# Forgetting attention with a channel mix on one core: norms of the first pairs spread by a selection matmul, a new layout for the later norms' trip, first mix from slot 5

## The chip, the cores and the metric

One core of one Trainium2 chip runs the whole program. The metric is the device time of one execution in microseconds. Runs are marked fast or slow by their time and clock. A ratio is the mean time of one kernel's fast runs over the mean time of the other's fast runs of the same rounds, so it is not quite the ratio of the medians that I quote: those are over all runs of a kernel, slow ones too. In the traces PE is TensorE's matmuls (PEld its weight loads), DVE is VectorE, ACT ScalarE, POOL GpSimd, and SPq the queue that issues the transfers.

## The reference, cut to what matters

```python
# q, k, v: (8 batches, 8 heads, 576, 64); f: (8, 8, 576)
scores = q @ k.T / 8 + cum[:, None] - cum[None, :]     # cum = cumsum(log(clip(f, 1e-4, 1)))
scores = where(causal, -1e9, scores)
x = softmax(scores) @ v                                # -> (8, 576, 512)
xk, xr = mixes of x and x shifted by one row (mu_k, mu_r)
out = sigmoid(xr @ w_r) * (relu(xk @ w_k) ** 2 @ w_v)  # (8, 576, 512), float32
```

The kernel folds the decay into v and into the softmax sums. What is left of the softmax is a division by a sum for each query, which is done on the way from PSUM to x.

## The kernel before

Heads are taken in 32 pairs. The main loop has 35 slots. Slot s computes the scores of pair s, the sums of pair s-1 and the values of pair s-3, with pieces of the channel mix in between. The sums of two pairs gather in one PSUM tile `den`. A "norm" turns the sums of such a group of two pairs into reciprocals R: 128 partitions of 288 values, of which two rows in every 32 are used. To scale x, each row must be spread over 64 partitions. This is done by a trip through DRAM:

```python
def norm(g):                       # after the sums of pairs 2g and 2g+1
    dT = dT_ring()
    nc.vector.transpose(dT..., den[:, 0:HQ])
    nc.vector.reciprocal(rt[:, :, 0:2], dT[:, :, 0:2])
    nc.vector.transpose(R..., rt...)

def spread_norm(g):                # scr: DRAM [4, 32, HQ]; HQ = 288
    scr = scr_ring()
    nc.sync.dma_start(out=scr.rearrange("g r c -> (g r) c"), in_=R.rearrange("p a b -> p (a b)"))
    rb = rb_ring()
    for half in range(2):
        for hh in range(2):
            nc.sync.dma_start(
                out=rb[hh * D:(hh + 1) * D, :, half * HQ:(half + 1) * HQ],
                in_=scr[2 * half + hh, 0:2, :].unsqueeze(0).to_broadcast([D, 2, HQ]))
    for i in range(2):
        rbs[2 * g + i] = rb[:, i, :]

def values(Pi, half):
    nm = mm_ring()                 # three PSUM buffers, shared with the mix
    ...                            # matmuls a x vw into nm
    nc.vector.tensor_tensor(out=xs[...], in0=nm[:, 0:HQ], in1=rbs[Pi][:, o:o + HQ], op=ALU.mult)
```

The channel mix comes in key units (x times w_k, `run_keys`, which take a buffer of the same `mm_ring`) and in gate and value blocks (w_r and w_v, `run_gv`). The order within a slot, cut:

```python
for s in range(NP + LAG):
    ...                            # loads
    scores(s, 0); mask(s, 0); scores(s, 1); mask(s, 1); mask(s, 4)
    run_gv(value_unit)
    transposes(s + 1)
    run_keys(2 * more)
    scores(s, 2); scores(s, 3); ...
    denominators(s - 1)
    values(Pi, 0); values(Pi, 1)   # Pi = s - 3
    ...
    if s % 2 == 0: norm(s // 2 - 1)
    run_keys(2 * more)
    if s % 2 == 0: spread_norm(s // 2 - 1)
    shift(Pi); run_gv(); ...
```

The softmax here doesn't subtract the row's maximum and nothing guards it: scores larger than these inputs give would overflow.

Of the kernel before, what the change touches and what calls it, by code (L numbers as in the profile page):

```python
# [9 lines left out]
F32 = mybir.dt.float32  # L10
# [18 lines left out]
HQ = 288  # L29
# [3 lines left out]
def kernel(  # L33
# [49 lines left out]
    scr_ring = Ring(2, [4, 32, HQ], F32, "scr", drp)  # L83
# [14 lines left out]

    NQ, NV = 3, 3
    qf = [cp.tile([P, 4, 2, D], F32, name=f"qf{i}") for i in range(NQ)]  # L100
    kf = [cp.tile([P, 4, 2, D], F32, name=f"kf{i}") for i in range(NQ)]
# [5 lines left out]
    def load(src, t, Pi, eng=None):  # L107
        b, h0 = divmod(2 * Pi, H)
        for hh in range(2):
            (eng or nc.sync).dma_start(  # L110
                out=t[:, :, hh, :],
                in_=src[b, h0 + hh, :4 * P, :].rearrange("(c p) d -> p c d", p=P))

    def load_qk(Pi):
        load(q, qf[Pi % NQ], Pi)
        load(k, kf[Pi % NQ], Pi)

    def load_v(Pi):
        load(v, vf[Pi % NV], Pi)

    def load_tail(i, b, eng=None):
        (eng or nc.sync).dma_start(out=tail_f[i],
                                   in_=(q, k, v)[i][b, :, 4 * P:, :].rearrange("h p d -> p h d"))

    for tt in tail[0] + tail[1]:
        nc.vector.memset(tt[64:, :, :], 0.0)
    for tt in tail[2]:
        nc.gpsimd.memset(tt[64:, :, :], 0.0)
# [4 lines left out]
    load_tail(0, 0)  # L133
    load_tail(1, 0, nc.scalar)
    nc.scalar.dma_start(out=lf, in_=f_bh[:, :])
    load_qk(1)
    mu_k_sb = cp.tile([P, n_db], F32)
# [3 lines left out]
    load_qk(2)  # L141
# [5 lines left out]
    make_identity(nc, ident32)  # L147
    NQK = 2
# [7 lines left out]
    nc.vector.memset(rt, 0.0)  # L156
    nc.gpsimd.memset(R, 0.0)
    den = dnp.tile([P, 512], F32)
# [10 lines left out]
    def cast_pair(Pi):  # L169
        res = []  # L170
        for ring, src in ((qb_ring, qf[Pi % NQ]), (kb_ring, kf[Pi % NQ])):
            t = ring()
            eng = nc.vector if Pi < 2 else nc.gpsimd
            eng.tensor_copy(t, src.rearrange("p c h d -> p c (h d)"))  # L174
            res.append(t)
        casts[Pi] = res

    def cast_tails(b):
        for i in range(2):
            eng = nc.vector if b == 0 else nc.gpsimd  # L180
            eng.tensor_copy(tail[i][b % 2][:64], tail_f[i])
# [13 lines left out]
    def transposes(Pi):  # L195
        b, p = divmod(Pi, PRW)
        tp = sc_ring().bitcast(BF16)
        for i, src in enumerate(casts.pop(Pi)):
            for c in range(NC):
                in_ = src[:, c, :] if c < 4 else \  # L200
                    tail[i][b % 2][:, 2 * p:2 * p + 2, :].rearrange("p h d -> p (h d)")
                nc.tensor.transpose(tp[:, i, c * P:(c + 1) * P], in_, ident)  # L202
        nc.vector.tensor_copy(qkT[Pi % NQK], tp[:, :, 0:640])  # L203

    cast_pair(0)
    cast_tails(0)
    transposes(0)



    ref = cp.tile([BH, 1], F32)
    nc.vector.memset(zrow, 0.0)
    nc.vector.tensor_scalar(lf, lf, scalar1=1e-4, scalar2=1.0, op0=ALU.max, op1=ALU.min)
    nc.scalar.activation(out=lf, in_=lf, func=AF.Ln)
    nc.vector.tensor_tensor_scan(out=cum, data0=lf, data1=zrow, initial=0.0,
                                 op0=ALU.add, op1=ALU.add)
    nc.vector.tensor_scalar(ref, cum[:, S - 1:S], scalar1=0.5, scalar2=None, op0=ALU.mult)
    nc.scalar.activation(out=wrow, in_=cum, func=AF.Exp, bias=ref, scale=-1.0)
    wtp = sc_ring()[:, 0, 0:NC * BH].rearrange("p (c h) -> p c h", c=NC)
    for c in range(NC):  # L220
        sz = P if c < 4 else 64
        nc.tensor.transpose(wtp[:sz, c, :], wrow[:, c * P:c * P + sz], ident32)
    nc.vector.tensor_copy(wbf[:, :4, :], wtp[:, :4, :])
    nc.vector.tensor_copy(wbf[:64, 4, :], wtp[:64, 4, :])


    for hh in range(2):
        for c in range(NC):
            nc.vector.tensor_copy(
                E[:, c, :].rearrange("p (g x) -> p g x", x=8)[:, :, hh * 2:hh * 2 + 6:5],  # L230
                wbf[:, c, :].rearrange("p (g h) -> p g h", h=4)[:, :, hh::2])
    cast_pair(1)


# [69 lines left out]
    def spread_norm(g):  # L304
        scr = scr_ring()
        nc.sync.dma_start(out=scr.rearrange("g r c -> (g r) c"),
                          in_=R.rearrange("p a b -> p (a b)"))
        rb = rb_ring()
        for half in range(2):
            for hh in range(2):  # L310
                nc.sync.dma_start(  # L311
                    out=rb[hh * D:(hh + 1) * D, :, half * HQ:(half + 1) * HQ],
                    in_=scr[2 * half + hh, 0:2, :].unsqueeze(0).to_broadcast([D, 2, HQ]))
        for i in range(2):
            rbs[2 * g + i] = rb[:, i, :]

# [129 lines left out]
    av_slot = {Pi: Pi + LAG for Pi in range(NP)}  # L446
    av_slot[NP - 1] -= 1
    mix_slot = [av_slot[b * PRW + PRW - 1] + 1 for b in range(B)]
    v_next = []
    for s in range(NP + LAG):  # L450
        if s in (3, 5, 6):
            load_weights((3, 5, 6).index(s))
        if s == 8:

            nc.vector.tensor_scalar(wv_sb, wv_sb, scalar1=0.5, scalar2=None, op0=ALU.mult)
        live = s < NP
        avs = [Pi for Pi in range(NP) if av_slot[Pi] == s]
        more = 1 if live else 2
# [8 lines left out]
        if s < NV:  # L467
            load_v(s)
# [3 lines left out]
        v_next = []  # L472
        if live:
            scores(s, 0)
            mask(s, 0)
            scores(s, 1)
            mask(s, 1)
            mask(s, 4)
        run_gv(value_unit)
        if s + 1 < NP:  # L480
            transposes(s + 1)
        if s in mix_slot:
            queue_mix(mix_slot.index(s))
        run_keys(2 * more)
        if live:
            scores(s, 2)
            scores(s, 3)
            mask(s, 2)
            mask(s, 3)
        if s + 2 < NP:  # L490
            cast_pair(s + 2)
            if (s + 2) % PRW == 0:
                cast_tails((s + 2) // PRW)
        if 0 <= s - 1 < NP:
            denominators(s - 1)
        for Pi in avs:
            values(Pi, 0)
            values(Pi, 1)
        for Pi in range(NP):
            if av_slot[Pi] - 1 == s:  # L500
                if Pi % PRW == 0:
                    vw_tail(Pi // PRW)
                vw_pair(Pi)
                v_next.append(Pi + NV)
        if 0 < s <= NP and s % 2 == 0:
            norm(s // 2 - 1)
        run_keys(2 * more)
        if 0 < s <= NP and s % 2 == 0:
            spread_norm(s // 2 - 1)
        for Pi in avs:  # L510
            if Pi % PRW == 0 and Pi >= 2 * PRW:
                finish_mix(Pi // PRW - 2)
            shift(Pi)
# [40 lines left out]
```

## Time and profile before

| | before |
|---|---|
| median of 3 runs | 354.72 us (354.68 to 356.07) |
| span of the profiled run | 353.4 us |
| PE busy | 281.1 us, 80% |
| DVE, ACT, POOL busy | 64%, 50%, 45% |
| first score matmul | 13.24 us |
| slot 5 starts, slot 11 starts | 49.42 us, 112.27 us |

A slot's start is its first score matmul in the timeline.

### The profile page before, as it was taken

Reading aid. Unit: us, or ns where it says so; the run is one execution under the profiler, and the core shown is the slowest. Engines: PE = TensorE matmul, PEld = TensorE weight load, DVE = VectorE, ACT = ScalarE, POOL = GpSimd, SP = SyncE. Lnnn points to the kernel's source line nnn. Section 1 sums busy time; section 2 is a strip of 40 time slices with the busy share of each in tenths; the row PEclk is TensorE's granted clock in tenths of the full one; section 3 lists DMA queues with packets and bytes.
Section 4 is the critical chain, followed back from the end, with each engine's and each line's share of the span. In section 5 each row is a group of like instructions: output and inputs, shape, how many; then the busy total and the mean of one; then the engine's idle time right before and its main releaser. Section 6 shows DMA issues by size and latency. Waiting matters only on the chain.

```text
span 353.4 us, 7425 instructions
## 1 busy us (share of the span) xinstructions
PE 281.1 (80%) x2725; PEld 163.9 (46%) x2725; DVE 225.7 (64%) x438; ACT 175.9 (50%) x296; POOL 159.5 (45%) x288
## 2 busy tenths in 40 slices
PE   1478256065989899889997989799979897997995
PEld 1244133043545455555554545455545554563652
DVE  5513171273867887886788867868888775587432
ACT  1564324025557475636574747456646565341541
POOL 2168456074546555744556455627574645100000
PEclk9999765558899999999999999999999999899999
DMA  9992987976888947796789669865969525031112
GB/s 159 193 187 56 194 155 113 210 160 143 137 168 155 227 111 174 183 222 130 168 201 189 149 151 204 198 152 134 222 139 200 145 64 171 30 105 60 70 59 89
DMA packets 134019, 52.80 MB, mean 149 GB/s; under 512 B 117024, under 2 KB 128800, under 8 KB 133984
## 3 DMA queue, kind: packets, MB, share of 16 engines
q1 hardware_dynamic: 130224, 49.18, 63.4%
q0 software_dynamic: 2096, 2.62, 4.9%
q10 hardware_dynamic: 1664, 0.54, 0.9%
q8 instruction: 21, 0.34, 0.4%
q14 instruction: 14, 0.11, 0.1%
HBM read 43.14 MB, written 11.80 MB: 155 GB/s over the span
## 4 chain that ended last, share of the span: by engine, by line
PE 48%; DMA 22%; DVE 21%; SPq 5%; issue 2%; ACT 2%; DVEq 0%; ACTq 0%
PE mm L374 19%; DMA rb<-scr 15%; PE mm L362 9%; DMA scr<-R 6%; PE mm L326 6%; DVE relusq L367 5%; SPq L311 5%; PE den L289 4%; PE sc L258 4%; PE sc L202 4%; DVE x L333 3%; DVE qkT L203 3%; DVE R L302 2%; DVE xr L351 2%; DVE dT L300 2%
## 5 line engine op out<-in xcount | busy, mean ns | idle before, releaser
L271 POOL TENSOR_SCALAR_AFFINE_SELECT a<-a 128x256 bf16<-128x256 bf16 (+1 forms) x160 | 71.9, 470 | 124.9 <-ACT a L264 111.0
L264 ACT ACTIVATE a<-sc 128x1024 bf16<-128x1024 f32 (+1 forms) x128 | 101.0, 836 | 41.8 <-PE sc L258 41.0
L366 ACT ACTIVATE rel<-mm 128x288 bf16<-128x288 f32 x128 | 52.5, 410 | 78.8 <-PE mm L362 76.0
L362 PE MATMUL mm<-xk,wk_sb 128*128 128x288 bf16 x512 | 75.8, 291 | 4.5 <-DVE x L333 3.9
L333 DVE TENSOR_TENSOR x<-mm,rb 128x288 bf16<-128x288 f32 x64 | 29.4, 462 | 65.8 <-DMA rb<-scr 43.2
L367 DVE TENSOR_TENSOR relusq<-rel 128x288 bf16<-128x288 bf16 x128 | 58.6, 481 | 12.7 <-ACT rel L366 10.5
L258 PE MATMUL sc<-qkT 64*128 64x64 bf16 (+4 forms) x384 | 41.3, 306 | 31.6 <-DVE qkT L203 30.2
L374 PE MATMUL mm<-wv_sb,relusq 128*128 128x512 bf16 x256 | 62.1, 383 | 5.0 <-DVE relusq L367 5.0
L362 PEld LDWEIGHTS <-wk_sb 128*128 128x128 bf16 x512 | 47.6, 99 | 20.9 <-issue 6.6
L258 PEld LDWEIGHTS <-qkT 64*128 64x128 bf16 x384 | 16.7, 99 | 60.2 <-issue 55.3
L388 ACT ACTIVATE th<-mm 128x512 f32<-128x512 f32 x36 | 21.5, 597 | 43.2 <-PE mm L374 35.8
L374 PEld LDWEIGHTS <-relusq 128*128 128x128 bf16 x256 | 23.6, 98 | 37.1 <-DVE relusq L367 7.4
L374 PE MATMUL mm<-wr_sb,xr 128*128 128x512 bf16 x128 | 33.7, 386 | 8.9 <-DVE x L333 8.9
L395 DVE SCALAR_TENSOR_TENSOR res<-th,mm 128x512 f32<-128x512 f32 x36 | 24.6, 683 | 25.2 <-ACT a L264 12.1
L184 POOL TENSOR_TENSOR vw<-vf,wbf 128x512 bf16<-128x512 f32 x32 | 33.8, 1058 | 1.5 <-DMA vf<-in_v_dram 1.5
L203 DVE COPY qkT<-sc 128x1280 bf16<-128x1280 bf16 x32 | 26.1, 816 | 11.1 <-PE sc L202 11.1
L326 PE MATMUL mm<-a,vw 128*64 128x288 bf16 (+3 forms) x448 | 30.3, 277 | 0.3 <-DVE x L333 0.3
L351 DVE SCALAR_TENSOR_TENSOR xk<-diff,mu_k_sb,x 128x576 bf16<-128x576 bf16 x32 | 27.0, 845 | 1.1
L351 DVE SCALAR_TENSOR_TENSOR xr<-diff,mu_r_sb,x 128x576 bf16<-128x576 bf16 x32 | 27.8, 867 | 0.0
L174 POOL CAST qb<-qf 128x512 bf16<-128x512 f32 x30 | 18.4, 613 | 13.8 <-DMA qf<-in_q_dram 13.8
L202 PE MATMUL sc<-ident,qb 128*128 128x128 bf16 x128 | 14.0, 240 | 12.2 <-ACT a L264 6.2
L289 PE MATMUL den<-a,E 128*2 128x288 bf16 (+4 forms) x512 | 23.5, 269 | 0.0
(55 smaller groups left out, 220.4 us busy)
## 6 DMA issues: line engine op xcount, KB each, us to landing
rb<-scr SPq DMA_DIRECT2D x64, 144.0 KB, 3.4
out_dram<-res SPq DMA_DIRECT2D x36, 256.0 KB, 3.4
qf<-in_q_dram SPq DMA_DIRECT2D x64, 128.0 KB, 3.6
vf<-in_v_dram SPq DMA_DIRECT2D x64, 128.0 KB, 3.6
kf<-in_k_dram SPq DMA_DIRECT2D x62, 128.0 KB, 3.8
scr<-R SPq DMA_DIRECT2D x16, 144.0 KB, 1.8
tail_f<-in_q_dram SPq DMA_DIRECT2D x8, 128.0 KB, 4.4
tail_f<-in_v_dram SPq DMA_DIRECT2D x8, 128.0 KB, 4.4
```

The lines of the kernel that those rows point to most:

```text
L203: nc.vector.tensor_copy(qkT[Pi % NQK], tp[:, :, 0:640])
L258: nc.tensor.matmul(sc[:, hh, w:w + n], lhsT=t[lo:lo + D, 1, kb * P:(kb + 1) * P], rhs=t[lo:lo + D, 0, q0:q0 + n], start=True, stop=True)
L264: nc.scalar.activation(out=a[:, :, off:off + w], in_=sc[:, :, 0:w], func=AF.Exp, scale=SCALE)
L271: nc.gpsimd.affine_select(out=v_, in_=v_, compare_op=ALU.is_ge, fill=0.0, base=0, pattern=[[0, 2], [1, n]], channel_multiplier=-1)
L289: nc.tensor.matmul(den[r0:r0 + 2, o:o + n], lhsT=E[:, kb, 2 * h:2 * h + 2], rhs=a[:, hh, col:col + n], start=(Pi % 2 == 0 and kb == 0), st ...
L326: nc.tensor.matmul(nm[hh * D:(hh + 1) * D, o:o + n], lhsT=t[:, kb, hh, :] if kb < 4 else tl[:, 2 * p + hh, :], rhs=a[:, hh, col:col + n], ...
L333: nc.vector.tensor_tensor(out=xs[Pi % NX][:, 1 + o:1 + o + HQ], in0=nm[:, 0:HQ], in1=rbs[Pi][:, o:o + HQ], op=ALU.mult)
L351: nc.vector.scalar_tensor_tensor(out=dst[:, p, :], in0=diff, scalar=mu[:, p:p + 1], in1=x[:, 0:S], op0=ALU.mult, op1=ALU.add)
L362: nc.tensor.matmul(kp[:, :HB], lhsT=wk_sb[:, db, fb * P:(fb + 1) * P], rhs=xks[b][:, db, hf * HB:(hf + 1) * HB], start=(db == 0), stop=(db ...
L366: nc.scalar.activation(rel, kp[:, :HB], func=AF.Relu)
L367: nc.vector.tensor_mul(rsq[b][:, fb, hf * HB:(hf + 1) * HB], rel, rel)
L374: nc.tensor.matmul(ps, lhsT=tiles[b][:, i, t0:t0 + P], rhs=w[:, i, :], start=(i == 0), stop=(i == n - 1))
```

## The change

Its intent is to shorten the first 100 us. The norms of the first four pairs are spread by a matmul with a matrix of ones and zeros instead of the trip. Values of these pairs come two slots after the scores instead of three, and their sums come first in a slot. q and k of the first six pairs are loaded in 1 KB runs (and put back in order by the qkT copy). The gate chain runs behind the first scores. The first mix starts in slot 5, and the weights are fetched two slots earlier. The later norms keep the trip, in a new DRAM layout with two reads instead of four. The diff, cut to its core:

```diff
-    scr_ring = Ring(2, [4, 32, HQ], F32, "scr", drp)
+    scr_ring = Ring(2, [64, 2, HQ], F32, "scr", drp)
+    RUNS = 6
+        if Pi < RUNS:
+            dma_start(out=t.rearrange("p (h x) -> p h x", h=2),
+                      in_=src[b, h0:h0 + 2, :4 * P, :].rearrange("h (p c) d -> p h (c d)", c=4))
 ...
     def spread_norm(g):
         scr = scr_ring()
-        nc.sync.dma_start(out=scr.rearrange("g r c -> (g r) c"),
+        nc.sync.dma_start(out=scr.rearrange("x f c -> f x c"),
                           in_=R.rearrange("p a b -> p (a b)"))
         rb = rb_ring()
-        for half in range(2):
-            for hh in range(2):
-                nc.sync.dma_start(
-                    out=rb[hh * D:(hh + 1) * D, :, half * HQ:(half + 1) * HQ],
-                    in_=scr[2 * half + hh, 0:2, :].unsqueeze(0).to_broadcast([D, 2, HQ]))
+        for hh in range(2):
+            nc.sync.dma_start(
+                out=rb[hh * D:(hh + 1) * D, :, :].rearrange("p j s -> p (j s)"),
+                in_=scr[32 * hh:32 * hh + 2, :, :].rearrange("j f c -> (j f c)")
+                    .unsqueeze(0).to_broadcast([D, 2 * S]))
+    def spread_now(Pi):
+        ...
+        for half in range(2):
+            rp = mm_ring()
+            nc.tensor.matmul(rp[:, 0:HQ], lhsT=sel[:, j, half, :], rhs=R..., start=True, stop=True)
+            nc.scalar.activation(out=rbs[Pi][:, half * HQ:(half + 1) * HQ], in_=rp[:, 0:HQ], func=AF.Copy)
 ...
+    FAST = 4
+    av_slot = {Pi: Pi + 2 if Pi < FAST else Pi + LAG for Pi in range(NP)}
+    n_keys = {5: (0, 2), 6: (2, 1), 7: (1, 2), 8: (2, 1), 9: (1, 2), 10: (1, 1)}
+    mix_slot[0] = 5
+    WEIGHTS = (1, 3, 4)                      # were slots 3, 5, 6
 ...
+        if ramp and s > 0:
+            denominators(s - 1)
+            if s % 2 == 0:
+                norm(s // 2 - 1)
+        if 0 < s - 1 <= FAST:
+            spread_now(s - 2)
```

More of the change, by code (lines that the diff above doesn't have):

```diff
@@ L95 @@
     res_ring = Ring(3, [P, Dm], F32, "res")
+    RUNS = 6
     NQ, NV = 3, 3
-    qf = [cp.tile([P, 4, 2, D], F32, name=f"qf{i}") for i in range(NQ)]
-    kf = [cp.tile([P, 4, 2, D], F32, name=f"kf{i}") for i in range(NQ)]
+    qf = [cp.tile([P, 8 * D], F32, name=f"qf{i}") for i in range(NQ)]
+    kf = [cp.tile([P, 8 * D], F32, name=f"kf{i}") for i in range(NQ)]
     vf = [cp.tile([P, 4, 2, D], F32, name=f"vf{i}") for i in range(NV)]
@@ L108, in load @@
         b, h0 = divmod(2 * Pi, H)
+        if Pi < RUNS:
+            (eng or nc.sync).dma_start(
+                out=t.rearrange("p (h x) -> p h x", h=2),
+                in_=src[b, h0:h0 + 2, :4 * P, :].rearrange("h (p c) d -> p h (c d)", c=4))
+            return
         for hh in range(2):
             (eng or nc.sync).dma_start(
-                out=t[:, :, hh, :],
+                out=t.rearrange("p (c h d) -> p h c d", c=4, h=2)[:, hh],
                 in_=src[b, h0 + hh, :4 * P, :].rearrange("(c p) d -> p c d", p=P))
@@ L118, in load_v @@
     def load_v(Pi):
-        load(v, vf[Pi % NV], Pi)
+        b, h0 = divmod(2 * Pi, H)
+        for hh in range(2):
+            nc.sync.dma_start(
+                out=vf[Pi % NV][:, :, hh, :],
+                in_=v[b, h0 + hh, :4 * P, :].rearrange("(c p) d -> p c d", p=P))
     def load_tail(i, b, eng=None):
@@ L123, in load_tail @@
                                    in_=(q, k, v)[i][b, :, 4 * P:, :].rearrange("h p d -> p h d"))
-    for tt in tail[0] + tail[1]:
-        nc.vector.memset(tt[64:, :, :], 0.0)
-    for tt in tail[2]:
-        nc.gpsimd.memset(tt[64:, :, :], 0.0)
     chain = [rb_ring() for _ in range(2)]
@@ L133 @@
     load_tail(0, 0)
+    nc.scalar.dma_start(out=lf, in_=f_bh[:, :])
     load_tail(1, 0, nc.scalar)
-    nc.scalar.dma_start(out=lf, in_=f_bh[:, :])
     load_qk(1)
+    load_v(0)
+    load_qk(2)
     mu_k_sb = cp.tile([P, n_db], F32)
@@ L140 @@
     nc.sync.dma_start(out=mu_r_sb, in_=moe_mu_r.rearrange("(db p) -> p db", p=P))
-    load_qk(2)
     ident = cp.tile([P, P], BF16)
@@ L147 @@
     make_identity(nc, ident32)
+    for tt in tail[0] + tail[1]:
+        nc.vector.memset(tt[64:, :, :], 0.0)
+    for tt in tail[2]:
+        nc.gpsimd.memset(tt[64:, :, :], 0.0)
     NQK = 2
@@ L155 @@
     R = cp.tile([P, 9, 32], F32)
-    nc.vector.memset(rt, 0.0)
+    nc.gpsimd.memset(rt, 0.0)
     nc.gpsimd.memset(R, 0.0)
+    sel = cp.tile([P, 2, 2, P], F32)
+    nc.gpsimd.memset(sel, 0.0)
+    for j in range(2):
+        for half in range(2):
+            for hh in range(2):
+                v_ = sel[:, j, half, hh * D:(hh + 1) * D]
+                nc.gpsimd.affine_select(
+                    out=v_, in_=v_, compare_op=ALU.not_equal, fill=1.0,
+                    base=-(32 * (2 * half + hh) + j), pattern=[[0, D]], channel_multiplier=1)
     den = dnp.tile([P, 512], F32)
@@ L173, in cast_pair @@
             eng = nc.vector if Pi < 2 else nc.gpsimd
-            eng.tensor_copy(t, src.rearrange("p c h d -> p c (h d)"))
+            if Pi < RUNS:
+                eng.tensor_copy(t.rearrange("p c (h d) -> p h c d", h=2),
+                                src.rearrange("p (h c d) -> p h c d", h=2, c=4))
+            else:
+                eng.tensor_copy(t, src.rearrange("p (c x) -> p c x", c=4))
             res.append(t)
@@ L193, in vw_tail, with transposes @@
             op=ALU.mult)
-    def transposes(Pi):
+    def transposes(Pi, parts=(range(NC),)):
         b, p = divmod(Pi, PRW)
         tp = sc_ring().bitcast(BF16)
-        for i, src in enumerate(casts.pop(Pi)):
-            for c in range(NC):
-                in_ = src[:, c, :] if c < 4 else \
-                    tail[i][b % 2][:, 2 * p:2 * p + 2, :].rearrange("p h d -> p (h d)")
-                nc.tensor.transpose(tp[:, i, c * P:(c + 1) * P], in_, ident)
-        nc.vector.tensor_copy(qkT[Pi % NQK], tp[:, :, 0:640])
@@ L205 @@
-    cast_pair(0)
-    cast_tails(0)
-    transposes(0)
+        for cs in parts:
+            for i, src in enumerate(casts[Pi]):
+                for c in cs:
+                    in_ = src[:, c, :] if c < 4 else                         tail[i][b % 2][:, 2 * p:2 * p + 2, :].rearrange("p h d -> p (h d)")
+                    nc.tensor.transpose(tp[:, i, c * P:(c + 1) * P], in_, ident)
+            lo, hi = cs[0] * P, (cs[-1] + 1) * P
+            t = qkT[Pi % NQK]
+            if Pi < RUNS and lo == 0:
+                nc.vector.tensor_copy(t[:, :, 0:4 * P].rearrange("p i (j c) -> p i j c", c=4),
+                                      tp[:, :, 0:4 * P].rearrange("p i (c j) -> p i j c", c=4))
+                lo = 4 * P
+            if lo < hi:
+                nc.vector.tensor_copy(t[:, :, lo:hi], tp[:, :, lo:hi])
+            if len(parts) > 1 and cs[-1] < NC - 1:
+                cast_tails(0)
@@ L211 @@
+        casts.pop(Pi)
     ref = cp.tile([BH, 1], F32)
     nc.vector.memset(zrow, 0.0)
+    cast_pair(0)
     nc.vector.tensor_scalar(lf, lf, scalar1=1e-4, scalar2=1.0, op0=ALU.max, op1=ALU.min)
     nc.scalar.activation(out=lf, in_=lf, func=AF.Ln)
-    nc.vector.tensor_tensor_scan(out=cum, data0=lf, data1=zrow, initial=0.0,
-                                 op0=ALU.add, op1=ALU.add)
-    nc.vector.tensor_scalar(ref, cum[:, S - 1:S], scalar1=0.5, scalar2=None, op0=ALU.mult)
-    nc.scalar.activation(out=wrow, in_=cum, func=AF.Exp, bias=ref, scale=-1.0)
@@ L219 @@
-    wtp = sc_ring()[:, 0, 0:NC * BH].rearrange("p (c h) -> p c h", c=NC)
-    for c in range(NC):
-        sz = P if c < 4 else 64
-        nc.tensor.transpose(wtp[:sz, c, :], wrow[:, c * P:c * P + sz], ident32)
-    nc.vector.tensor_copy(wbf[:, :4, :], wtp[:, :4, :])
-    nc.vector.tensor_copy(wbf[:64, 4, :], wtp[:64, 4, :])
-    for hh in range(2):
-        for c in range(NC):
-            nc.vector.tensor_copy(
-                E[:, c, :].rearrange("p (g x) -> p g x", x=8)[:, :, hh * 2:hh * 2 + 6:5],
-                wbf[:, c, :].rearrange("p (g h) -> p g h", h=4)[:, :, hh::2])
@@ L232, with forget_gates, forget_weights @@
-    cast_pair(1)
+    transposes(0, (range(4), range(4, NC)))
+    def forget_gates():
+        nc.vector.tensor_tensor_scan(out=cum, data0=lf, data1=zrow, initial=0.0,
+                                     op0=ALU.add, op1=ALU.add)
+        nc.vector.tensor_scalar(ref, cum[:, S - 1:S], scalar1=0.5, scalar2=None, op0=ALU.mult)
+        nc.scalar.activation(out=wrow, in_=cum, func=AF.Exp, bias=ref, scale=-1.0)
+    def forget_weights():
+        wtp = mm_ring()[:, 0:NC * BH].rearrange("p (c h) -> p c h", c=NC)
+        for c in range(NC):
+            sz = P if c < 4 else 64
+            nc.tensor.transpose(wtp[:sz, c, :], wrow[:, c * P:c * P + sz], ident32)
+        nc.vector.tensor_copy(wbf[:, :4, :], wtp[:, :4, :])
+        nc.vector.tensor_copy(wbf[:64, 4, :], wtp[:64, 4, :])
+        for hh in range(2):
+            for c in range(NC):
+                nc.vector.tensor_copy(
+                    E[:, c, :].rearrange("p (g x) -> p g x", x=8)[:, :, hh * 2:hh * 2 + 6:5],
+                    wbf[:, c, :].rearrange("p (g h) -> p g h", h=4)[:, :, hh::2])
@@ L305, in spread_norm @@
         scr = scr_ring()
-        nc.sync.dma_start(out=scr.rearrange("g r c -> (g r) c"),
+        nc.sync.dma_start(out=scr.rearrange("x f c -> f x c"),
                           in_=R.rearrange("p a b -> p (a b)"))
         rb = rb_ring()
-        for half in range(2):
-            for hh in range(2):
-                nc.sync.dma_start(
-                    out=rb[hh * D:(hh + 1) * D, :, half * HQ:(half + 1) * HQ],
-                    in_=scr[2 * half + hh, 0:2, :].unsqueeze(0).to_broadcast([D, 2, HQ]))
+        for hh in range(2):
+            nc.sync.dma_start(
+                out=rb[hh * D:(hh + 1) * D, :, :].rearrange("p j s -> p (j s)"),
+                in_=scr[32 * hh:32 * hh + 2, :, :].rearrange("j f c -> (j f c)")
+                    .unsqueeze(0).to_broadcast([D, 2 * S]))
         for i in range(2):
             rbs[2 * g + i] = rb[:, i, :]
+    def spread_now(Pi):
+        g, j = divmod(Pi, 2)
+        if j == 0:
+            rb = rb_ring()
+            for i in range(2):
+                rbs[2 * g + i] = rb[:, i, :]
+        for half in range(2):
+            rp = mm_ring()
+            nc.tensor.matmul(rp[:, 0:HQ], lhsT=sel[:, j, half, :],
+                             rhs=R.rearrange("p a b -> p (a b)"), start=True, stop=True)
+            nc.scalar.activation(out=rbs[Pi][:, half * HQ:(half + 1) * HQ], in_=rp[:, 0:HQ],
+                                 func=AF.Copy)
     def values(Pi, half):
@@ L445, with attend, shifted, weigh @@
     LAG = 3
-    av_slot = {Pi: Pi + LAG for Pi in range(NP)}
+    FAST = 4
+    av_slot = {Pi: Pi + 2 if Pi < FAST else Pi + LAG for Pi in range(NP)}
     av_slot[NP - 1] -= 1
     mix_slot = [av_slot[b * PRW + PRW - 1] + 1 for b in range(B)]
+    n_keys = {5: (0, 2), 6: (2, 1), 7: (1, 2), 8: (2, 1), 9: (1, 2), 10: (1, 1)}
+    mix_slot[0] = 5
+    WEIGHTS = (1, 3, 4)
+    def attend(Pi):
+        values(Pi, 0)
+        values(Pi, 1)
+    def shifted(Pi):
+        if Pi % PRW == 0 and Pi >= 2 * PRW:
+            finish_mix(Pi // PRW - 2)
+        shift(Pi)
+    def weigh(Pi):
+        if Pi % PRW == 0:
+            vw_tail(Pi // PRW)
+        vw_pair(Pi)
     v_next = []
     for s in range(NP + LAG):
-        if s in (3, 5, 6):
-            load_weights((3, 5, 6).index(s))
-        if s == 8:
+        if s in WEIGHTS:
+            load_weights(WEIGHTS.index(s))
+        if s == 6:
             nc.vector.tensor_scalar(wv_sb, wv_sb, scalar1=0.5, scalar2=None, op0=ALU.mult)
@@ L457 @@
         avs = [Pi for Pi in range(NP) if av_slot[Pi] == s]
+        ramp = bool(avs) and avs[0] < FAST or s < FAST
         more = 1 if live else 2
@@ L466 @@
             load_tail(2, s // PRW)
-        if s < NV:
+        if 0 < s < NV:
             load_v(s)
@@ L475 @@
             mask(s, 0)
+            if s == 0:
+                forget_gates()
             scores(s, 1)
@@ L478 @@
             mask(s, 4)
+        if 0 < s - 1 <= FAST:
+            spread_now(s - 2)
+        if s == FAST + 1:
+            attend(FAST - 1)
+            shifted(FAST - 1)
         run_gv(value_unit)
         if s + 1 < NP:
+            if s == 0:
+                cast_pair(1)
             transposes(s + 1)
@@ L483 @@
             queue_mix(mix_slot.index(s))
-        run_keys(2 * more)
+        nk = n_keys.get(s, (2 * more, 2 * more))
+        run_keys(nk[0])
         if live:
@@ L489 @@
             mask(s, 3)
+        if s == 0:
+            forget_weights()
         if s + 2 < NP:
@@ L493 @@
                 cast_tails((s + 2) // PRW)
-        if 0 <= s - 1 < NP:
+        if not ramp and 0 <= s - 1 < NP:
             denominators(s - 1)
-        for Pi in avs:
-            values(Pi, 0)
-            values(Pi, 1)
+        if s != FAST + 1:
+            for Pi in avs:
+                attend(Pi)
         for Pi in range(NP):
             if av_slot[Pi] - 1 == s:
-                if Pi % PRW == 0:
-                    vw_tail(Pi // PRW)
-                vw_pair(Pi)
+                weigh(Pi)
                 v_next.append(Pi + NV)
-        if 0 < s <= NP and s % 2 == 0:
+        if not ramp and 0 < s <= NP and s % 2 == 0:
             norm(s // 2 - 1)
-        run_keys(2 * more)
-        if 0 < s <= NP and s % 2 == 0:
+        run_keys(nk[1])
+        if 2 * FAST // 2 < s <= NP and s % 2 == 0:
             spread_norm(s // 2 - 1)
-        for Pi in avs:
-            if Pi % PRW == 0 and Pi >= 2 * PRW:
-                finish_mix(Pi // PRW - 2)
-            shift(Pi)
+        if s != FAST + 1:
+            for Pi in avs:
+                shifted(Pi)
         run_gv()
```

## The prediction

> **What bounds the kernel now.** I read the slices first: PE is 8 or 9 tenths busy from the tenth slice on, but far less in the first nine (80 us). So I asked for the busy time between the starts of successive slots; a slot is one turn of the main loop, and I took its start from the first score matmuls in the timeline. Columns: window, length, then PE, PEld, DVE, ACT, POOL busy us, PE clock, DMA share, GB/s.
>
> ```profile
> 0.00:13.20 13.20, 1.81 (x12) 1.14 (x13) 7.16 (x20) 4.02 (x4) 2.29 (x11) 1.00 1.10 169
> ...
> 23.60:28.75 5.15, 4.03 (x43) 2.23 (x40) 0.82 (x1) 3.13 (x4) 2.95 (x8) 1.00 0.51 82
> 28.75:35.40 6.65, 5.52 (x60) 3.31 (x58) 2.05 (x4) 3.13 (x4) 6.64 (x12) 1.00 0.32 76
> 35.40:49.40 14.00, 4.79 (x56) 2.87 (x54) 4.12 (x7) 3.24 (x4) 7.30 (x14) 0.65 0.94 183
> 49.40:56.80 7.40, 4.69 (x60) 2.91 (x58) 4.38 (x8) 3.24 (x4) 4.95 (x9) 0.73 0.92 154
> 56.80:75.40 18.60, 5.44 (x56) 3.28 (x54) 4.48 (x7) 3.24 (x4) 6.88 (x12) 0.50 0.93 174
> ...
> 104.70:113.60 8.90, 8.90 (x93) 5.17 (x93) 6.97 (x13) 6.47 (x11) 4.51 (x10) 1.00 1.05 180
> ```
>
> The last row is slot 10: PE works all of it. Slots 4 and 6 take 14.0 and 18.6 us with about 5 us of PE work in each. Nothing computes before 13.2 us. The chain of waits over the first 100 us says why:
>
> ```profile
> 12.07 0.78 ACT rb L218
> ...
> 30.26 1.75 DMA scr<-R
> ...
> 33.96 9.32 DMA rb<-scr
> ...
> 51.43 5.42 DMA scr<-R
> ...
> 58.82 10.11 DMA rb<-scr
> ```
>
> The reciprocal sums R go to DRAM and come back spread over 64 partitions. The trip costs about 13 us (30.26 to 43.28) and 17.5 us (51.43 to 68.93), because the rings hold loads and 2 MB weight reads (DMA share 0.92 to 0.94 in those slots). Later the same trip takes 1.74 us out, 2.5 us to issue four reads and 3.9 us for the last of them (129.99 to 137.57). The waits for 100 to 300 us show what that still costs (engine, producer, total us, times, longest):
>
> ```profile
> DVE x L333 <- DMA rb<-scr: 12.3, 9, 2.4
> ...
> PE mm L374 <- DVE x L333: 7.0, 7, 2.2
> ...
> PE mm L362 <- DVE x L333: 1.2, 2, 0.9
> ```
>
> So there are two bounds: the trip and the late start in the first 80 us, then PE, about 90% busy, at 8.8 to 8.9 us a slot. From slot 11 (113.6 us) to the end are 353.4 - 113.6 = 239.8 us.
>
> **What the Trainium skill says.** (1) "TensorE: Matmul & The Clock Gate", Part 1: an array idle or sparsely used runs at half clock and needs about 3.4 us of sustained work for the full one. The trace agrees: four transposes take 0.58 us at 58.56 (after idling) and 0.39 at 97.62. (2) "FP8 and Floating Point Precision", TensorE Precision Notes: a true FP32 matmul makes four passes. No row of this trace tests a 288-column one. (3) "VectorE: DVE Perf Modes", What auto-detection actually checks: the doubled rate wants 16-bit data at step 1. The plain qkT copy agrees: 1280 elements in 0.816 us, 1.57 per ns. (4) "DMA: Bandwidth & Descriptors", Why a DMA increments its semaphore by 16 and not by 1: the engines used are the largest number up to 16 that divides the slowest dimension of both sides. The rb trip agrees with full width now (144 KB landing in 1.75 us), but see the first rival.
>
> **The change part by part.**
>
> *Start.* The first scores leave the shadow of the gate chain (clip, Ln, scan, Exp, transposes). In the timeline qkT of pair 0 is copied at 8.03 to 8.85, the scores start at 13.24. The clip of f still stands before that copy, as does the load, but q and k arrive in 1 KB runs. I take 8.8 us for the first scores: 13.2 - 8.8 = 4.4 us gained. The gate chain then runs inside slot 0, which I lengthen from 5.3 to 6.0 us (five transposes and twelve small copies, some 1.6 us of DVE, partly beside the exponentials).
>
> *Slot 1.* The sums now come first in a slot, so they wait for the masks of the slot before, about 1.2 us (exponential end 23.2 to mask end 23.9, against PE free at 22.7). 5.1 becomes 6.5 us.
>
> *Slots 2 to 4.* PE takes over values two slots after the scores instead of three: 1.7 us each at half clock. The spread is two FP32 matmuls of 288 columns a pair: by four passes at 1.2 GHz, 4 x 288 / 1.2 = 0.96 us each, 1.9 us a pair cold, about 1 warm (estimate from page 2 and 1). ACT copies each out as the rel row does, 0.41 us. DVE's permuting qkT copy of 1024 strided elements at 1 per cycle of 0.96 GHz is 1.07 us, plus a small copy and overheads, about 1.45 against 0.82 us (estimate from page 3). Cold, PE has 4.25 (slot 2 now, scores, transposes, sums) + 1.76 + 1.9 = 7.9 us; warm, about 5. ACT has 3.1 + 0.8 us, DVE at most 1.45 + 1.25 (norm) + 0.92 + 2.1 = 5.7 us. I choose 7.3 us a slot: 22 us for three. Slot 5 then starts at 8.8 + 6.0 + 6.5 + 22 = 43.3 us instead of 49.4.
>
> *Slots 5 to 10.* They must hold the whole first mix, which stood in slots 7 to 10. PE per slot at full clock: transposes 0.62, scores 1.3, sums 0.65, values 1.06, together 3.6 us; six slots 21.6. Sixteen key units at 4 x 0.144 us = 9.2. Four gate and value blocks at 1.03 + 1.90 = 11.7, of which I count 10. That is 41 us; at the steady 90% 45, and I give 48 for small waits, weights among them. Slot 11 starts at 91.3 instead of 113.6: **22 us gained**, the 14.0 and 18.6 us slots being the source.
>
> *Transfers.* A 256 B packet costs 25 ns of an engine (159 GB/s at share 0.98 in the first 9 us); a 2 KB one about 87 (64 GB/s at share 0.17 after 320 us, where only results go out). A straight line puts 1 KB at 52 ns against 4 x 25. Six pairs of q and k are 3.1 MB: at 163 GB/s 19 us of full DMA, at about 318 GB/s 10: 9 us of load off the ramp, with 4 us more for two trips that are gone. Demand up to slot 4, which I add up to some 50 us, weights brought forward included, then fits the computation's 43 us only just: DMA becomes the near rival.
>
> *Later norms.* Fourteen groups still take the trip, with two 4.6 KB-row reads instead of four. That saves two issues (1.3 us) and some drain, unless the write is slower. With full width this could save up to the 8.2 us that PE waits for x; with rival A it would cost.
>
> Sum: 354.7 - 22 = 332.7 us before the last item, which I set to zero on balance. **Predicted 333 us**.
>
> **The rivals.**
>
> A. *The write of R becomes narrow.* Its DRAM side now has the halves (2) as slowest dimension. By page 4 that means two engines: 64 packets of 1152 B each at some 56 ns (from the same line), 3.6 us instead of 0.5, so 4.9 us to land. Both halves of rb then come at about 138 where the first half is now used at 136.07 us. PE would stop 1.0 to 1.5 us longer in each of some 13 groups, 13 to 20 us, and most of the gain is given back: 346 to 350 us. For it: the page and the shape. Against: the two issues saved, and that the access may be carried in another order. I give it 35%. If instead all 16 engines serve it, 326 us.
>
> B. *Transfers bound the ramp.* Weights start in slots 1, 3, 4 instead of 3, 5, 6, and the scaling of wv, in slot 6, would hold DVE until its 2 MB land (13 us now). For it: share 0.93 in slots 4 and 6. Against: the 13 us of DMA saved. It would cost 3 to 8 us: 336 to 341.
>
> C. *PE stays cold in slots 0 to 4 and the FP32 spread with it*, plus the slower copy: 8.3 instead of 7.3 us a slot, 336 us. Or PE warms earlier: 330.
>
> D. *The ramp was hidden anyway.* Against: slots 11 to 34 do the same work as before, nothing in them waits for the earlier start to be absorbed, and PE is the bound there. I give it almost no weight.
>
> **Range and chances.** 333 with the ramp's own error of 6 us, one rival lifting it to 348, and a wide spread lowering it to 326, gives 322 to 347 for 8 in 10. Two per cent is 7.1 us, that is, faster means below 347.6: 0.90. Within 2%: 0.08, rival A with B. Slower: 0.02.
>
> **What would show it.** First score matmul near 8.8 us (not 13.2). No wait of x for rb before slot 6, and no gap of PE beyond 3 us between 15 and 60 us. Slot 5 near 43, slot 11 near 91 us, and then 240 us to the end. The spread matmuls at about 0.5 to 1 us each; the first qkT copies at 1.1 to 1.3 us. q and k loads at half the packets, DMA share under 0.95 in slots 1 to 5. The landing time of the R write decides rival A: 1.8 us or about 5. The prediction is wrong if that time is long and x waits for it in every group, or if DVE stands at the wv scaling for several us.

## The result

The changed kernel takes 404.23 us (median of 4 runs, 401.53 to 406.58) against 354.7 us (354.01 to 356.07). The ratio of the fast runs is 1.1388 (1.1288 to 1.1489): it is 14% slower. PE is busy 303.8 us of a span of 404.9.

The same view as in the prediction, busy time by slots, for the changed kernel. The rows are the time to the first scores, slots 3, 4, 5, 7 and 13:

```profile
0.00:9.26 9.26, 1.68 (x11) 0.91 (x12) 5.76 (x17) 3.25 (x3) 5.29 (x21) 1.00 0.87 193
...
32.19:38.84 6.65, 4.27 (x63) 2.98 (x60) 5.82 (x8) 3.74 (x6) 6.64 (x12) 1.00 0.40 57
38.84:49.55 10.71, 5.67 (x62) 3.84 (x59) 6.48 (x11) 4.06 (x6) 5.21 (x10) 0.84 1.17 188
49.55:58.64 9.09, 5.97 (x54) 3.63 (x51) 6.82 (x11) 4.26 (x7) 5.54 (x9) 0.88 1.09 204
63.97:82.24 18.27, 11.68 (x82) 5.85 (x83) 6.09 (x12) 5.38 (x10) 9.01 (x16) 0.72 0.77 133
...
131.61:145.45 13.84, 9.17 (x91) 5.08 (x91) 7.01 (x14) 5.24 (x9) 5.43 (x9) 0.87 0.71 127
```

The first scores start at 9.26 us instead of 13.24. Slot 4 takes 10.7 us, where it took 14.0, and no long slot stands ahead of slot 7. (The clock column's 1.00 in the first slots can't be right: four transposes take 0.63 us at 27.79 and 0.39 at 33.80, and it says 1.00 for both. By these times PE runs slow, or cold, up to slot 2.) But slot 11 starts only at 109.67 us (before: 112.27), and from there to the end are 295.2 us instead of 241.1. So the loss lies from slot 7 on, mostly in the steady slots, where I had expected no change. Slot 13 shows it: 13.8 us for 9.2 us of PE. The chain of waits through that slot:

```profile
130.83 0.48 DVE R L340
131.31 0.03 DVE relusq L419
131.34 5.26 DMA scr<-R
136.60 0.02 issue
136.62 0.48 SPq L348
137.10 0.05 issue
137.15 4.54 DMA rb<-scr
...
142.18 0.47 DVE x L385
142.65 0.04 issue
142.69 1.12 PE mm L414 x4
```

The same trip in the kernel before:

```profile
129.99 1.74 DMA scr<-R
...
133.68 3.89 DMA rb<-scr
...
137.69 0.47 DVE x L333
```

From R to x are 10.9 us (131.31 to 142.18). In the kernel before it was 7.7 us (129.97 to 137.69) for the later half of x, and the first half was multiplied at 136.07 already. The write takes 5.26 us where it took 1.74. The reads land later, not sooner, although there are two of them. PE stops for 4.43 us ahead of its four matmuls at 142.69: the two halves of the values and one key unit hold the three buffers of `mm_ring`, and the next key unit gets one only when x has been read out. After the gap those four take 1.12 us where four such take 0.66 us at full clock. The clock column (third from the right) says 0.50 there. And while the write runs, the share of the 16 DMA engines that is busy (second from the right) is 0.14, about two of them:

```profile
142.69:146.00 3.31, 3.09 (x11) 1.29 (x13) 2.20 (x6) 0.85 (x2) 0.00 (x0) 0.50 1.37 199
133.00:133.50 0.50, 0.50 (x8) 0.26 (x6) 0.50 (x1) 0.50 (x2) 0.20 (x1) 1.00 0.14 41
```

The waits of the whole span (engine, producer, total us, times, longest):

```profile
DVE x L385 <- DMA rb<-scr: 69.5, 14, 6.5
...
PE mm L414 <- DVE x L385: 46.3, 13, 4.9
...
PE mm L378 <- DVE x L385: 4.9, 1, 4.9
```

On average PE stands 3.6 us in each of 13 groups.

### The profile page after: what moved, and what is told of

Same layout as the page of the kernel before. It is cut to its first block, busy times and chain, and to the rows that moved or that the text cites. A ratio compares the mean times of both kernels' runs of the same rounds, so it can differ in the third digit from the quotient of the medians.

```text
span 404.9 us, 7392 instructions
## 1 busy us (share of the span) xinstructions
PE 303.8 (75%) x2717; PEld 171.2 (42%) x2741; DVE 229.6 (57%) x443; ACT 179.6 (44%) x304; POOL 162.9 (40%) x298
## 4 chain that ended last, share of the span: by engine, by line
PE 43%; DMA 34%; DVE 14%; issue 4%; ACT 2%; SPq 2%; POOL 1%; ACTq 0%; DVEq 0%; POOLq 0%
PE mm L426 18%; DMA rb<-scr 16%; DMA scr<-R 16%; PE mm L414 9%; PE sc L296 4%; DVE x L385 4%; PE mm L378 4%; PE sc L229 3%; PE den L327 3%; DVE R L340 2%; DMA tail_f<-in_k_dram 2%; SPq L348 2%; DVE qkT L233 2%; DVE dT L338 1%; ACT a L302 1%
## 5 line engine op out<-in xcount | busy, mean ns | idle before, releaser
L414 PE MATMUL mm<-xk,wk_sb 128*128 128x288 bf16 x512 | 83.0, 304 | 48.0 <-DVE x L385 46.3
L385 DVE TENSOR_TENSOR x<-mm,rb 128x288 bf16<-128x288 f32 x64 | 28.1, 460 | 79.8 <-DMA rb<-scr 69.5
L426 PE MATMUL mm<-wv_sb,relusq 128*128 128x512 bf16 x256 | 68.5, 413 | 4.0 <-DVE relusq L419 4.0
L419 DVE TENSOR_TENSOR relusq<-rel 128x288 bf16<-128x288 bf16 x128 | 54.4, 438 | 25.6 <-ACT rel L418 23.7
L426 PEld LDWEIGHTS <-relusq 128*128 128x128 bf16 x256 | 25.5, 106 | 42.4 <-issue 16.1
L426 PE MATMUL mm<-wr_sb,xr 128*128 128x512 bf16 x104 | 39.3, 459 | 3.1 <-issue 2.4
L378 PE MATMUL mm<-a,vw 128*64 128x288 bf16 (+3 forms) x448 | 29.1, 269 | 5.5 <-DVE x L385 4.9
L237 DVE COPY qkT<-sc 128x1280 bf16<-128x1280 bf16 (+1 forms) x32 | 22.9, 716 | 3.7 <-PE sc L229 3.6
L378 PEld LDWEIGHTS <-vw 128*64 128x64 bf16 x448 | 19.5, 113 | 10.9 <-issue 6.6
L426 PEld LDWEIGHTS <-xr 128*128 128x128 bf16 x128 | 14.5, 115 | 16.1 <-issue 7.1
```

The source lines that it names most:

```text
L378: nc.tensor.matmul(nm[hh * D:(hh + 1) * D, o:o + n], lhsT=t[:, kb, hh, :] if kb < 4 else tl[:, 2 * p + hh, :], rhs=a[:, hh, col:col + n], ...
L385: nc.vector.tensor_tensor(out=xs[Pi % NX][:, 1 + o:1 + o + HQ], in0=nm[:, 0:HQ], in1=rbs[Pi][:, o:o + HQ], op=ALU.mult)
L414: nc.tensor.matmul(kp[:, :HB], lhsT=wk_sb[:, db, fb * P:(fb + 1) * P], rhs=xks[b][:, db, hf * HB:(hf + 1) * HB], start=(db == 0), stop=(db ...
L419: nc.vector.tensor_mul(rsq[b][:, fb, hf * HB:(hf + 1) * HB], rel, rel)
L426: nc.tensor.matmul(ps, lhsT=tiles[b][:, i, t0:t0 + P], rhs=w[:, i, :], start=(i == 0), stop=(i == n - 1))
```

## The experiments

Theory T: the write of R, whose DRAM side has 2 as its slowest dimension, lands late, and since x waits for it in every second slot the lateness is lost time. Its rivals: the rearranged start, weights and mix cost the time (W); the two long reads are to blame (R); the busy engines hold up other loads. All runs gave correct results. They ran in four groups (e1 to e4, e5 to e8, e9 to e12, e13 and later), each beside the kernel before on its chip: 354.24, 354.95, 355.83 and 355.98 us. Groups are compared through that.

### e1: the old trip in the changed kernel

```diff
-    scr_ring = Ring(2, [64, 2, HQ], ...)      # and the changed spread_norm
+    scr_ring = Ring(2, [4, 32, HQ], ...)      # and the spread_norm of before
```

> The changed kernel with only the trip of R put back (flat write of 128 rows, four reads). Theory T (the narrow write, 5.25 us instead of 1.75 us to land, is what eats the gain): 325 to 340 us, the write lands in 1.8 us again, x waits for rb at most 15 us in all. Rival W (weights moved forward, fewer key units per slot or the FP32 spread cost the time): still above 370 us, with slots 7 to 10 still long.

340.35 us (338.37 to 344.35), ratio to before 0.9591 (0.9515 to 0.9668). One function put back turns 14% slower into 4% faster. Its waits and PE's total:

```profile
DVE x L385 <- DMA rb<-scr: 15.6, 13, 2.2
...
PE mm L426 <- DVE x L385: 7.6, 8, 1.8
...
PE mm L414 <- DVE x L385: 0.9, 2, 0.5
...
PE mm L378 <- DVE x L385: 0.4, 1, 0.4
```

```profile
PE 280.8 (83%) x2741; PEld 164.3 (49%) x2741; DVE 233.8 (69%) x443; ACT 178.8 (53%) x304; POOL 163.0 (48%) x298
```

The changed kernel's PE waits for x 51.2 us (46.3 + 4.9), this one 8.9 (7.6 + 0.9 + 0.4): 42.3 us of difference. Its PE is busy 303.8 us for the same work that takes 280.8 here: 23.0 us, which go with the clock that falls after gaps (0.898 on average, here 0.979; that alone would make 280.8 us into 306). Together 65.3 us, and the two profiled spans differ by 68.2 (404.9 and 336.7); the changed kernel's trace also lacks 24 of 2741 PE records, which leaves 2.4 us counted as idle. So both terms of the loss are found. W falls; 340.35 lies just past the far edge of what T said, 340. Which parts of the change bring the 14 us that are left is tested for two of them only (e8, e9).

### e2: the new trip in the kernel before

The diff is the reverse of e1's, made in the kernel before.

> The kernel before with only the new trip of R. Theory T: 395 to 425 us (13 to 16 groups each about 4 us longer, and the clock falling after each gap). Rival W: within 10 us of before, 345 to 365.

410.08 us (407.06 to 414.87), ratio 1.1551 (1.1462 to 1.1639). The trip alone, with nothing else of the change, costs 55 to 56 us. T holds.

### e3, e4 and e7: write and reads apart

e3 keeps the layout and the two reads, and cuts the write into two of 64 rows:

```diff
-        nc.sync.dma_start(out=scr.rearrange("x f c -> f x c"), in_=R...)
+        for f_ in range(2):
+            nc.sync.dma_start(out=scr[:, f_, :], in_=R[64 * f_:64 * f_ + 64]...)
```

> The changed kernel with its write of R cut into two transfers of 64 rows, same bytes in the same places, same two reads. Theory T (it is the width of the write): the write lands in about 2 us, 325 to 345 us. Rival R (the two long-row reads, which take 4.2 us to land in the changed kernel, are as much to blame): 360 to 385 us.

356.7 us (353.2 to 361.64), ratio 1.0039 (0.994 to 1.0138). Each write lands in 2.0 us. This is better than T's rival and worse than T: the write carries most, not all.

e4 keeps the narrow write and reads four half rows:

```diff
-        for hh in range(2):                       # two reads of 4.6 KB rows
+        for half in range(2):
+            for hh in range(2):
+                nc.sync.dma_start(out=rb[hh * D:(hh + 1) * D, :, half * HQ:(half + 1) * HQ],
+                    in_=scr[32 * hh:32 * hh + 2, half, :].unsqueeze(0).to_broadcast([D, 2, HQ]))
```

> The changed kernel with its narrow write kept, but four reads of half rows as before. Theory T: write 5.2 us, total 395 to 415 us, little better or worse than the changed kernel. Rival R: 350 to 375 us, as the reads were the trouble.

398.46 us (395.09 to 401.4), ratio 1.1279 (1.1188 to 1.1369). With the write narrow, the reads matter by some 6 us only, and the intervals of the two ratios overlap.

e7 joins both edits, the write in two and four reads in the new layout:

> As e3 (write of the new layout in two wide transfers), but four half-row reads instead of two reads of 4.6 KB rows. If the long reads, of which both are needed before either half of x can be scaled, cost e3 its 16 us over e1 (Theory L): 338 to 347 us. If it is the second write (Rival): 352 to 360, as e3.

344.92 us (343.0 to 347.35), ratio 0.9731 (0.9656 to 0.9806). So of e3's 16 us over e1, the long reads carry about 12 (356.7 to 344.9) and the second write the rest, some 4 us, which is hardly clear of the noise. The issue table of e3 has its two reads landing after a median of 4.0 us, that of e7 its four after 3.4. With two reads by head neither half of x can be scaled until both have landed; with four, the first half can go ahead. The runs don't separate these two reasons.

### e5 and e6: the width of the write as a dose

Both are e1 with a padded DRAM tile, so that the slowest dimension of the write is 4 or 8 and can't merge with the next:

```diff
-    scr_ring = Ring(2, [4, 32, HQ], ...)          # write: 128 rows, flat
+    scr_ring = Ring(2, [4, 33, HQ], ...)          # e5; write out=scr[:, 0:32, :]
+    scr_ring = Ring(2, [8, 17, HQ], ...)          # e6; write out=scr[:, 0:16, :]
```

> As e1 (old reads), but the write's DRAM side is padded so that its slowest dimension is 4 and can't be merged with the next. If the engines used are the largest divisor up to 16 of that dimension (Theory T), each of 4 engines takes 32 rows: a line through the two landing times known, 1.75 us at 8 rows an engine and 5.25 at 64, gives 1.25 + 0.0625 x 32 = 3.25 us. Total 352 to 372 us. Rival S (any three-dimensional, strided write is slow, whatever its width): 5 us to land and about 395 us. Rival N (padding changes nothing): 1.8 us and 340.

> The same with a slowest dimension of 8: by Theory T 16 rows an engine, 1.25 + 0.0625 x 16 = 2.25 us to land, total 342 to 355 us. Rival S: 5 us and about 395. Rival N: 1.8 us, 340.

The writes in the chains of waits (start, us), first e1, then slowest dimension 8, 4 and 2 (e4). Under each stands a stretch of its trace in which only such a write runs; the share of the 16 DMA engines is second from the right:

```profile
115.09 1.75 DMA scr<-R
...
133.60:134.10 0.50, 0.50 (x3) 0.20 (x2) 0.50 (x2) 0.50 (x2) 0.50 (x2) 1.00 0.83 295
```

```profile
122.60 2.76 DMA scr<-R
...
141.60:142.60 1.00, 1.00 (x6) 0.29 (x3) 1.00 (x1) 1.00 (x2) 1.00 (x2) 1.00 0.48 134
```

```profile
120.48 3.57 DMA scr<-R
...
141.60:143.40 1.80, 1.11 (x6) 0.29 (x3) 1.80 (x1) 1.42 (x2) 1.80 (x2) 1.00 0.26 78
```

```profile
127.27 5.26 DMA scr<-R
...
150.80:154.40 3.60, 2.50 (x20) 1.30 (x19) 3.56 (x5) 1.50 (x2) 3.60 (x5) 1.00 0.13 40
```

By "DMA: Bandwidth & Descriptors", section Why a DMA increments its semaphore by 16 and not by 1, the last three run on 8, 4 and 2 engines, with 16, 32 and 64 rows of 1152 B for each. The shares agree: 0.48, 0.26 and 0.13 of 16 are 7.7, 4.2 and 2.1 engines, and in e1 0.83 is 13, where the page gives 16. So the width is seen in the traces and not only inferred from times. From 16 to 32 rows the time grows by 0.81 us and from 32 to 64 by 1.69: 51 and 53 ns a row. That is a straight line, as rows that queue on so few engines would give; I had estimated 56 ns. Its start, 2.76 - 16 x 0.052 = 1.93 us, lies above what e1's 1.75 us gives less 8 such rows (1.33). So these three-dimensional writes take some 0.6 us more than the line of rows explains, about half of it in the issue (0.63 and 0.57 against 0.34 us on the queue); the other half I did not trace. I had not foreseen that (both landed later than the 2.25 and 3.25 us that I expected), and Rival S holds to this small part.

e6 takes 355.17 us (353.35 to 356.38), ratio 1.0012 (0.9941 to 1.0083); e5 368.88 (364.67 to 372.37). Two of e5's four runs were slow, so fast runs alone are compared here: their means are 339.7 us (e1), 355.0 (e6), 365.1 (e5) and 397.3 (e4). Against e1, e6 loses 15 us for 1.0 us of lateness in 14 groups, e5 25 for 1.8, and e4 58 for 3.5. Each microsecond of lateness costs about 1.0 to 1.2 us a group from the first on. There was no slack at all in the trip where it stood.

### e8 and e9: two other parts of the change taken out

e8 is e1 with `RUNS = 0`, so q and k come in 256 B runs as before. e9 is e1 with `mix_slot[0] = 7` and `n_keys = {}`.

> As e1, but q and k of the first six pairs in 256 B runs as before, so the qkT copy of those pairs is one plain copy again (0.82 us instead of 1.22 + 0.28). My prediction's account (9 us of DMA load saved, 0.6 us of DVE a slot paid): 342 to 350 us, slot 1 and 2 starting later by 1 to 3 us. Rival (the loads were hidden): 334 to 340 us, faster than e1, because the copy stands in the chain of each slot.

> As e1, but the first mix is queued in slot 7 with the key counts of the kernel before (4 a slot). My prediction takes the gain of the early mix as part of the 22 us, without a share: I expect 344 to 352 us, since slots 5 and 6 are then short but slots 7 to 10 are PE-bound at 8.8 us again. Rival (the early mix buys nothing, the trip alone counted): 336 to 342.

e8: 342.28 us (339.92 to 345.18), ratio 0.9631 (0.9534 to 0.9727), which overlaps e1's; it lies at the edge between the two expectations. Slot 5 starts at 49.27 us, in e1 at 49.09. The 1 KB runs do load more (259 instead of 194 GB/s in the second 10 us), but nothing waited for it. e9: 336.7 us (335.09 to 337.88), ratio 0.9485 (0.9441 to 0.9529). The early mix brought nothing; it may even cost a little: slot 11 starts at 93.03 us, in e1 at 97.87. My expectation for e9 was wrong and its rival right.

### e10 and e11: the order of the ramp, and the norm early

e10 is e1 with two changes of order. The sums of pair 0 stand behind the first scores of slot 1, and the shift of pair 1 behind the norm of slot 4:

```diff
-        if ramp and s > 0:
+        if ramp and s > 1:
             denominators(s - 1)
             if s % 2 == 0:
                 norm(s // 2 - 1)
+        if s == FAST:
+            shifted(1)                # was at the end of slot 3
 ...
+        if s == 1:
+            denominators(0)           # behind scores(1, 0) and scores(1, 1)
```

> As e1, with two waits of its ramp taken out by order alone: the sums of pair 0 stand behind the first scores of slot 1 (they waited for the copies of E), and the norm of slot 4 stands ahead of the shift of pair 1 (PE waited 3.8 us for R). If these waits carried the 5.8 us by which my slots 0 to 4 were too short: 334 to 338 us, slot 5 at 44 to 46 instead of 49.1 us. If other waits take their place: 338 to 342.

337.12 us (334.86 to 337.94), ratio 0.9476 (0.9432 to 0.952). Slot 5 starts at 44.66 us, 4.4 earlier than in e1; some 3 us of it reach the end. Most of it comes from slot 4 (6.4 us instead of 10.8).

e11 adds this, for even slots from 6 on:

```diff
+        early = not ramp and 0 < s <= NP and s % 2 == 0
+        if early:
+            denominators(s - 1)       # before scores(s, 0)
 ...                                   # behind transposes(s + 1):
+        if early:
+            norm(s // 2 - 1)
+            spread_norm(s // 2 - 1)   # both were late in the slot
```

> As e10, with the sums of even slots from 6 on at the start of the slot and the norm and trip behind the qkT copy, about 2 us earlier. x then waits for rb hardly at all (under 4 us in all, 15.6 in e1), PE gains up to the 7.6 us that it waited for x: 326 to 334 us. If DVE's norm in front of other work costs as much as it gains: 334 to 340.

325.25 us (322.21 to 329.63), ratio 0.9137 (0.9096 to 0.9177). The waits are those of the second time that it ran (e11 again, below):

```profile
PE mm L414 <- DVE x L385: 2.5, 10, 0.3
DVE x L385 <- DMA rb<-scr: 2.1, 3, 0.9
PE mm L426 <- DVE x L385: 1.1, 3, 0.4
```

x waits 2.1 us for rb in the whole run, where e1 has 15.6. From e10 to e11 are 12 us, a little more than I had expected at most (326).

### e12: the narrow write, early

This is the changed kernel as it is, narrow write and long reads and all, with e11's edit placed right at the start of the slot.

> The changed kernel with its narrow write and its two long reads as they are, but in even slots from 6 on the sums, the norm and the trip stand at the start of the slot, some 4 to 5 us earlier for the same work. Theory T says the 404 us come from the trip's latency on the path to x, and not from the transfers it loads: then the time falls to 335 to 360 us, with x waiting for rb 20 us at most in all. Rival (the two busy DMA engines hold up the loads behind them): it stays above 380 us.

339.83 us (337.67 to 342.63), ratio 0.9567 (0.9515 to 0.9619). Its waits:

```profile
DVE x L385 <- DMA rb<-scr: 11.9, 7, 4.6
...
PE mm L414 <- DVE x L385: 5.7, 6, 1.8
```

The same transfers, some microseconds sooner, and 64 us are back. So what costs is the trip's latency on the path to x, and not the load that two busy engines put on the others. The slow trip is not free even so: e11, with the old trip and e10's order, is 15 us faster.

### e13, e14 and e11 again: what was still open

e13 puts e11's edit into the kernel before and nothing else. e14 is e11 with the late mix of e9. e11 ran again beside it.

> The kernel before with nothing changed but the place of the sums, the norm and the trip in even slots (as in e11). If the steady slots' waits are what it removes: about 10 us, 342 to 348 us (e11 against e10 was 12). If the two long trips of slots 4 and 6 also start early enough to be hidden in part: 330 to 342.

> As e11, with the first mix from slot 7 as before. If the early mix is worth nothing (as e9 says, which was no slower than e1): 321 to 328 us. If it fills idle PE time once the trip is hidden: 328 to 334, slower than e11.

> The same kernel as e11, for the same chip as e14: 322 to 328 us.

e13: 337.02 us (336.06 to 343.12), ratio 0.9514 (0.9436 to 0.9592). The place of the norm alone is worth 19 us in the kernel before, more than all that e1 keeps of the change (17 us by the fast runs alone; the verdict on record is unclear). Slot 4 is short with it (6.0 us instead of 14.0), slot 6 still takes 17.6. Of the 18.7 us between the profiled spans, 8.4 are gained by slot 11 (103.92 against 112.27) and the rest after it. e14: 323.3 us (321.09 to 326.19), ratio 0.9153 (0.9088 to 0.9218); e11 again 324.92 us (323.26 to 330.96), 0.9165 (0.9108 to 0.9222). The late mix and the early one can't be told apart. e11 and e14 beat both kernels by a wide margin.

## Why the prediction was wrong

I had 333 us and a range of 322 to 347; it is 404.23. The step that failed is the item "Later norms", which I "set to zero on balance", and in it **the size of rival A**. Its mechanism was right: "two engines", "4.9 us to land" (5.26 measured), first shown by the landing time, as I had asked, and by a DMA share of 0.13 to 0.14 during the write. The terms that were mis-sized:

- **The cost per group.** I wrote that PE would stop "1.0 to 1.5 us longer in each of some 13 groups, 13 to 20 us". The runs show 58 us (medians) for the narrow write alone (e4 against e1), 4.1 us in each of 14 groups, and 64 us with the long reads. I had netted off two saved issues and "some drain" of the reads. I had rb complete at about 138, 8.0 us after the write's start; it came after 10.4 (131.34 to 141.69). The reads took 4.54 us after the last issue in that chain, not the 2.5 us or so that this needed. And I took the waits of 7.0 and 1.2 us in the trace as a sign that the trip was mostly hidden. It was just about in time, without slack: each microsecond later costs 1.0 to 1.2 us (e4 to e6).
- **The clock.** I cited "TensorE: Matmul & The Clock Gate", Part 1, and didn't carry it into the rival. The trace agrees with the page: after the 4.43 us gap of PE in slot 13 the granted clock is 0.50 up to 146 us. With such stretches PE is busy 23 us longer in the changed kernel than in e1.
- **Its weight.** The page stated a rule, the shape was plain in the diff, and I gave it 35%.

Point by point on the rest:

- *Start:* 8.8 us, measured 9.26. Right.
- *Slots 0 to 4:* 34.5 us, measured 40.6 in e1. Slot 0 took 8.7 instead of 6.0, since the sums of pair 0, which stand ahead of slot 1's first scores, fall in it and waited 1.4 us for the gate chain's copies; slot 4 took 10.8 instead of 7.3, since DVE reached the norm late and PE waited 3.8 us for R. In e10 these slots take 35.3 us.
- *Spread:* "1.9 us a pair cold, about 1 warm", measured 2.29 and 1.24. The permuting copy: 1.22 + 0.28 us, "about 1.45". Right.
- *Slots 5 to 10:* 48 us, measured 48.8 in e1. Right as a sum. Its cause was wrong: the early mix is no part of the gain (e9, e14).
- *Gain of the ramp:* 22 us, measured 14.4 at slot 11 of e1 (97.87 against 112.27) and 14 in the medians. My slot 11 of before, 113.6 us, was itself 1.3 us late. With the trip left as it was, the time is e1's 340 us, within the range.
- *Transfers:* the 9 us of DMA load saved were hidden (e8). Rival B did not come: the scaling of wv waited for nothing.
- *Rivals C and D:* PE was cold in slots 0 to 2 and warm in slot 3 (its four transposes 0.39 us), so C came in part. D did not: e1 keeps at the end the 14 us that it has gained at slot 11.
- *What would show it:* slot 11 to the end "240 us" was the line that the trace refuted, 295.2. Two smaller signs failed too: PE stopped 3.8 us once before 60 us (for R, in slot 4), and the DMA share was 1.17 and 1.09 in slots 4 and 5.
- *Slips in the working:* slot 2's PE time is given as 4.25 us, but the row shows 4.03; the tenth slice is still at 5 tenths; and 333 us plus rival A's 13 to 20 are 346 to 353, not 350.

## What to carry to other kernels

Before touching a transfer that something waits for in every round, ask how late it may come: here one microsecond of latency in a 144 KB write cost one microsecond or a little more in each of fourteen rounds, though the bytes of a trip stayed the same and its transfers fell from five to three. Read the slowest dimension of both sides of a DMA before its bytes. And before making such a trip faster, see whether what starts it can stand earlier in the program: moving the sums and the norm up within the slot was worth 12 to 19 us, and brought even the kernel with the slow trip from 404 to 340 us.

## What the Trainium skill lacked or had wrong

- "DMA: Bandwidth & Descriptors", Why a DMA increments its semaphore by 16 and not by 1: the rule on the number of engines agrees with four writes of the same bytes (1.75, 2.76, 3.57 and 5.26 us; DMA shares 0.83, 0.48, 0.26 and 0.13). The page gives no time for a write on few engines: here 51 to 53 ns a row of 1152 B on each engine, to DRAM.
- No page that I read has the extra time of a three-dimensional DRAM side: some 0.6 us to land beyond the rows, of which 0.2 to 0.3 us in the issue (0.55 to 0.63 against 0.34 us).
- "DMA: Bandwidth & Descriptors", Rules for kernel authors, advises to coalesce many small transfers, above all those under 64 KB (these are of 144 and 288 KB), and says nothing of what a consumer can start on. Two reads of 4.6 KB rows landed in 4.0 us and four of half rows in 3.4, and the kernel with the two was 12 us slower (e3 against e7), whether by the later landing or because with four the consumer could begin after half of them, the runs don't separate.
- "FP8 and Floating Point Precision", TensorE Precision Notes, four passes for FP32: two matmuls of 288 columns took 2.29 us cold and 1.24 us warm, 19 to 29% above the estimate from four passes (1.92 and 0.96 us). The trace shows each as two instructions.
